# Decode attention, two blocks: all query weights first, output weights last, and a TensorE loop

## The chip, the cores and the metric

The kernel runs on one core of one Trainium2 chip. The metric is device time in microseconds, the median of several runs; lower is better.

## The reference, cut to what matters

Two blocks, A and B, of the same shape do the same work on their own inputs, and their results stand side by side in the output.

```python
B, Sq, D = 2, 1, 640
H, Sk, Dh = 32, 8192, 192          # bfloat16 everywhere
q = (x @ wq).reshape(B, Sq, H, Dh).transpose(0, 2, 1, 3)        # x: 2x1x640, wq: 640x6144
scores = einsum("bhqd,bhkd->bhqk", q, k_cache) * Dh ** -0.5      # k_cache: 2x32x8192x192
p = softmax(scores, axis=-1)
o = einsum("bhqk,bhkd->bhqd", p, v_cache)
block = o.transpose(0, 2, 1, 3).reshape(B, Sq, H * Dh) @ wo      # wo: 6144x640
out = concatenate([block_A, block_B], axis=-1)
```

Each K and each V cache has 201 MB; each wq and each wo has 7.86 MB. Every byte of them is read once, 836.77 MB in all, and there is one query per head.

## The kernel before

**Units.** Work goes by units. A unit is one batch element and two heads; block A has units 0 to 31 and block B units 32 to 63. Partitions 0 to 63 hold the first head, 64 to 127 the second, and each partition holds 128 positions of 192 values, so that one K (or V) load is 128 rows of 49,152 bytes, 6.29 MB. Two units, the two batch elements of a pair of heads, make a pair `hp`.

**Buffers and loads.** Three buffers `kv` take K and V in turn. SP issues all large loads from one queue in the order of the list `loads`: K of unit u+1 ahead of V of unit u, with the last two K ahead of the last three V. A load waits until the load three places before it has been used up: a K buffer is free after the fourth multiply of its unit (`("m", u, 3)`), a V buffer after its PV product (`("pv", u)`). One buffer `wbuf` holds the weights of eight heads at a time: wq of a window of eight heads (`sp_wq`, five rows of 3,072 bytes per partition) and wo of the window (`sp_wo`, four rows of 3,840 bytes per partition) alternate in it. They stand in SP's queue between the K loads, wq behind the sixth K of a window of eight units and wo behind the fourth of the next. The last window's wo comes as four loads after the last V.

**A unit's work.** TensorE makes the query of a unit, repeated over the partitions, with five matmuls (`pe_q`, L294), and ScalarE copies it to SBUF (`act_a0`, L277). VectorE multiplies K by the query in four chunks (`dve_mul`, L219). TensorE sums each product over 192 values as far as 16 with twelve matmuls against an identity (`pe_sum`, L302), VectorE does the rest (`dve_red`, L222) and takes the maximum (L228). GpSimd makes the maximum common to all partitions (L211). ScalarE takes the exponentials into `pb` (L252) with their sums in `rs`; GpSimd adds these over the partitions (L214) and VectorE inverts them (L236). TensorE multiplies by V with 64 matmuls, two positions at once (`pe_pv`, L312).

**Output.** For each pair, ScalarE copies the PV result out (`act_f1`, L261), TensorE turns it across partitions (`pe_f3`, L322), ScalarE scales it by the inverse sum (`act_f4`, L268), and for each window TensorE multiplies it by wo (`pe_f5`, L335), six matmuls a pair, each pair waiting for the one before it.

**Order.** The program is written out by hand: `put` places each operation in a slot and an order within it, and `_Stream.emit` writes each engine's list out in full, with the semaphore waits that remain. TensorE's slot u holds the sums of unit u and after them the PV product of unit u-1.

## Time and profile before

| what | value |
|---|---|
| time, median of 3 runs | 1975.02 us (1973.26 to 1975.65) |
| the profiled execution, first to last instruction (span) | 1972.4 us |
| moved by DMA | 837.99 MB, mean 425 GB/s |
| large loads, share of 16 DMA engines | 98.8% |
| program code, q8 | 66 packets, 1.08 MB |
| TensorE matmuls busy | 1576.7 us, 8448 of them |
| VectorE, ScalarE, GpSimd busy | 1067.3, 196.5 and 60.2 us |

The page comes from one execution, and its own time is the span; the 2.6 us between span and median lie outside the instructions. Times are from the span's start. GB/s and busy tenths are given for 40 equal slices of the span. In a group or timeline line the output stands left of the arrow and the inputs right of it, then the form and the count; a bracket gives the engine's idle time before it and who ended that. Beside the views, the trace holds a record of each DMA packet (start, length, bytes) and of each of the sixteen parts in which a load reports that it has landed.

### The profile page before, as it was taken

The page shows a single profiled execution, that of the slowest core. Times are in us where ns is not written, and L with a number is a line of the kernel's source. Part 1 is how long each engine was busy: PE and PEld are TensorE (multiplying, and loading weights), DVE is VectorE, ACT ScalarE, POOL GpSimd, SP SyncE. Part 2 cuts the span into 40 slices and gives each one's busy share as a digit, 9 for nine tenths or more (in the row PEclk, how much of TensorE's full clock was granted, in tenths as well). Part 3 has the DMA queues.
Part 4 walks back from the last instruction along what each step waited for, and adds up shares of the span by engine and source line. Part 5 has one row for each costly group of instructions (what it writes and reads, how often), then busy time and mean ns, then how long its engine had stood idle before and what let it go on. Part 6 is the DMA issues. An engine that isn't in the chain of part 4 may idle for free.

```text
span 1972.4 us, 18847 instructions
## 1 busy us (share of the span) xinstructions
PE 1576.7 (80%) x8448; PEld 773.3 (39%) x8448; DVE 1067.3 (54%) x772; ACT 196.5 (10%) x647; POOL 60.2 (3%) x145
## 2 busy tenths in 40 slices
PE   3887888878788788787887878878788777878769
PEld 1443434434344343343443434434344333443325
DVE  5664565545654555546556455464554655645570
ACT  0110110001000011000110101100011001110001
POOL 1000000000000000000000000000000000000000
PEclk9999998999999899998998989999999999999889
DMA  9999999999999999999999999999999999999996
GB/s 404 432 432 431 431 429 434 431 427 433 433 427 428 433 430 433 431 426 437 430 430 431 426 433 431 433 431 427 434 433 431 427 429 427 433 433 428 426 380 275
DMA packets 29345, 837.99 MB, mean 425 GB/s; under 512 B 3016, under 2 KB 3024, under 8 KB 12624
## 3 DMA queue, kind: packets, MB, share of 16 engines
q1 hardware_dynamic: 28676, 836.77, 98.8%
q8 instruction: 66, 1.08, 0.2%
q10 hardware_dynamic: 588, 0.01, 0.0%
q14 instruction: 15, 0.12, 0.0%
HBM read 836.77 MB, written 0.01 MB: 424 GB/s over the span
## 4 chain that ended last, share of the span: by engine, by line
DMA 50%; PE 28%; DVE 19%; issue 3%; ACT 0%; SPq 0%
DMA kv<-in_B_k_cache_dram 24%; DMA kv<-in_A_k_cache_dram 24%; PE ops L312 18%; DVE prod L219 17%; PE scps L302 9%; DVE sc L222 2%; DMA kv<-in_B_v_cache_dram 2%; PE outps L335 0%; PE qps L322 0%; PE qps L294 0%; DVE mp L228 0%; SPq L178 0%; ACT qbc L277 0%; DVE rcT L236 0%; ACT out_sb L282 0%
## 5 line engine op out<-in xcount | busy, mean ns | idle before, releaser
L219 DVE TENSOR_TENSOR prod<-kv,qbc 128x6144 bf16<-128x6144 bf16 x256 | 852.7, 3352 | 637.0 <-DMA kv<-in_B_k_cache_dram 320.3
L302 PE MATMUL scps<-prod,ident 128*128 128x512 bf16 x3072 | 775.2, 409 | 355.4 <-DVE prod L219 355.3
L312 PE MATMUL ops<-kv,pb 128*34 128x384 bf16 x4096 | 676.6, 326 | 2.2 <-DMA kv<-in_B_v_cache_dram 1.1
L302 PEld LDWEIGHTS scps<-prod,ident 128*128 128x128 bf16 x3072 | 301.3, 104 | 821.8 <-DVE prod L219 455.3
L312 PEld LDWEIGHTS ops<-kv,pb 128*34 128x34 bf16 x4096 | 395.6, 98 | 274.9 <-issue 15.5
L222 DVE TENSOR_REDUCE sc<-scps 128x32 f32<-128x512 f32 x256 | 175.8, 687 | 204.1 <-PE scps L302 204.1
L244 ACT ACTIVATE nb<-mg 64x1 f32<-64x1 f32 x128 | 25.7, 201 | 1314.3 <-POOL mg L211 1313.5
L294 PE MATMUL qps<-wbuf,xbc 128*128 128x384 bf16 x320 | 64.7, 334 | 34.4 <-ACT qbc L277 24.5
L252 ACT ACTIVATE pb<-sc,nb 64x128 bf16<-64x128 f32 x128 | 81.7, 638 | 31.9 <-PE ops L312 28.8
L211 POOL PARTITION_ALL_REDUCE mg<-mp x64 | 26.0, 406 | 1717.9 <-DVE mp L228 1717.9
L277 ACT ACTIVATE qbc<-qps 64x192 bf16<-64x192 f32 x128 | 41.6, 325 | 181.8 <-PE qps L294 180.6
L294 PEld LDWEIGHTS qps<-wbuf,xbc 128*128 128x128 bf16 x320 | 26.5, 99 | 69.8 <-ACT qbc L277 36.8
L261 ACT ACTIVATE o_sb<-ops 2x384 f32<-2x384 f32 (+1 forms) x66 | 31.1, 471 | 223.9 <-PE ops L312 223.5
L322 PEld LDWEIGHTS qps<-sel,o_sb 34*64 34x64 f32 x768 | 36.3, 171 | 13.6 <-issue 13.4
L322 PE MATMUL qps<-sel,o_sb 34*64 34x1 f32 x768 | 39.1, 225 | 0.0
L252 ACT ACTIVATION_READ_ACCUMULATOR pb<-sc,nb 64x1 f32 x128 | 38.6, 301 | 0.0
L228 DVE TENSOR_REDUCE mp<-sc 64x1 f32<-64x128 f32 x128 | 35.9, 280 | 3.1
L236 DVE RECIPROCAL rcT<-lall 64x1 f32<-64x1 f32 x128 | 20.1, 157 | 25.4 <-POOL lall L214 22.5
L214 POOL PARTITION_ALL_REDUCE lall<-rs x64 | 27.9, 436 | 157.6 <-ACT pb L252 157.6
L335 PE MATMUL outps<-wbuf,oTz 128*4 128x320 bf16 x192 | 31.3, 299 | 1.4
L335 PEld LDWEIGHTS outps<-wbuf,oTz 128*4 128x4 bf16 x192 | 13.7, 84 | 16.3 <-PE outps L335 8.9
L268 ACT ACTIVATE oTz<-qps,rcT 128x3 bf16<-128x3 f32 x64 | 13.7, 268 | 15.5 <-PE qps L322 14.7
(19 smaller groups left out, 15.8 us busy)
## 6 DMA issues: line engine op xcount, KB each, us to landing
kv<-in_A_k_cache_dram SPq DMA_DIRECT2D x32, 6144.0 KB, 30.3
kv<-in_A_v_cache_dram SPq DMA_DIRECT2D x32, 6144.0 KB, 30.1
kv<-in_B_k_cache_dram SPq DMA_DIRECT2D x32, 6144.0 KB, 30.5
kv<-in_B_v_cache_dram SPq DMA_DIRECT2D x30, 6144.0 KB, 30.4
kv<-in_B_v_cache_dram SPq DMA_DIRECT2D x3, 3072.0 KB, 13.0
wbuf<-in_A_wq_dram SPq DMA_DIRECT2D x4, 1920.0 KB, 33.3
wbuf<-in_A_wo_dram SPq DMA_DIRECT2D x4, 1920.0 KB, 33.1
wbuf<-in_B_wq_dram SPq DMA_DIRECT2D x4, 1920.0 KB, 32.9
```

Of the source, the lines that this page charges most:

```text
L214: return lambda eng: eng.partition_all_reduce(lall[u % 2][:], rs[u % 2][:], 128, bass.bass_isa.ReduceOp.add)
L219: return lambda eng: eng.tensor_tensor(prod[c % 2][:], t[:, c * TC:(c + 1) * TC, :], q, ALU.mult)
L222: return lambda eng: eng.tensor_reduce(sc[u % 2][:, c * TC:(c + 1) * TC], scps[c % 2][:], AXL.X, ALU.add)
L228: ins = eng.tensor_reduce(mp[u % 2][r, s:s + 1], sc[u % 2][r, :], AXL.X, ALU.max)
L252: ins = eng.activation(pb[u % 2][r, :, s::32], sc[u % 2][r, :].rearrange("p (j a) -> p j a", a=2), ACTF.Exp, bias=nb[u % 2][r, :], scale=s ...
L261: ins = eng.activation(o_sb[r, b0:b1, :], ops[hp % 2][r, b0:b1, a * Dh:(a + 1) * Dh], ACTF.Identity)
L277: ins = eng.activation(qbc[u % NQ][r, :], qps[r, s * Dh:(s + 1) * Dh], ACTF.Identity)
L294: ins = eng.matmul(qps[:, 0:QW], xbc[b][:, c, :], wq_t[:, c, off:off + QW], start=(c == 0), stop=(c == DC - 1))
L302: ins = eng.matmul(scps[c % 2][:], ident[:], prod[c % 2][:, :, j * DG:(j + 1) * DG], start=(j == 0), stop=(j == NJ - 1))
L312: ins = eng.matmul(ops[(u // B) % 2][0:MP, u % B, 0:QW], pb[u % 2][:, j, :], vv[:, j, :], start=(j == 0), stop=(j == TJ - 1))
L322: ins = eng.matmul(oTps[64 * s:64 * s + 64, 2 * i + b:2 * i + b + 1], o_sb[:, b, :].rearrange("p (r i) -> p i r", i=3)[:, i, :], sel[:, s: ...
L335: ins = eng.matmul(outps[0:4, 0:NH2], oTz[:, hp % NZ, i, 2 - 2 * half:6 - 2 * half], wo_t[:, hp % PW, i, half * NH2:(half + 1) * NH2], sta ...
```

## The change

- **wq first.** The whole wq of block A and that of block B are loaded at the start, each in one transfer, one row of 61,440 bytes per partition (`ld_wq`). They lie in one large tile `big`, in the place that the K/V buffers and the products take later. All 32 pairs' queries are made before the first unit: `pe_q` now makes both batch elements of a pair with five matmuls, VectorE (`dve_qx`) and ScalarE (`act_q`) copy them into `qall`. The first two K loads wait for block A's queries, the first V for all.
- **wo last.** wo comes in eight pieces (`pieces`, `ld_wo`) with rows of 30,720 bytes down to 2,560. The first, half of block A's, goes to the last K's buffer and stands in SP's queue ahead of the last V; the others follow the last V. K and V alternate to the end.
- **Outputs.** A unit's PV result is added up and scaled by VectorE and ScalarE and written over the unit's query in `qall`. The sums of the exponentials come from one small matmul (`pe_l`) in place of GpSimd's. At the end TensorE turns each block's outputs with 64 matmuls against `place` (`pe_turn`) and multiplies them by wo with 96 (`pe_out`).
- **Loop.** `_find` looks for the longest stretch of slots that repeats every six; TensorE's list has the slots 3 to 62 as a loop of ten turns, in which each wait is for a register times a step plus a constant. The slots before and after, and the other engines' lists, are written out.

The diff, cut to its core:

```diff
+    def emit(self, eng, period=None):
+        ops = self.resolve()
...
+        first, plen, reps, steps = self._find(ops, period)
+        self._emit(eng, ops[:first])
+        with eng.Fori(0, reps) as it:
+            self._emit(eng, ops[first:first + plen], it, steps)
+        self._emit(eng, ops[first + plen * reps:])
...
+    def _emit(self, eng, ops, it=None, steps=None):
+        for fn, need, has_sig, _ in ops:
+            for sid, (sem, val) in need.items():
+                eng.wait_ge(sem, val if it is None else it * steps[sid] + val)
...
-        wbuf = sb("wbuf", [128, DC * HW * Dh], BF16)
+        big = sb("big", [128, NBUF * BUFE + 2 * PRODE], BF16)
+        qall = sb("qall", [128, NU, Dh], BF16)
...
-        for u in (LASTU - 1, LASTU):
-            loads.remove(("k", u))
-            loads.insert(loads.index(("v", LASTU - 3)), ("k", u))
...
+        pieces = [
+            (0, 0, HWR, woA, [("m", LASTU, NCH - 1)]),
+            (0, HWR, WR, woA + HWR * D, [("s", LASTU, NCH - 1)]),
+            (1, 0, 16, b62 * BUFE, [("pv", LASTU - 1)]),
+            (1, 16, 32, b62 * BUFE + 16 * D, []),
+            (1, 32, 40, b63 * BUFE, [("pv", LASTU, 0)]),
+            (1, 40, 44, b63 * BUFE + 8 * D, []),
+            (1, 44, 46, b63 * BUFE + 12 * D, []),
+            (1, 46, 48, b63 * BUFE + 14 * D, []),
+        ]
...
+        def ld_wq(blk):
+            src = blocks[blk]["wq"].rearrange("(j c) n -> j (c n)", c=DC)
+            return dma(big[:, wq_off[blk]:wq_off[blk] + WQE], src, ("wq", blk))
+
+        def ld_wo(n):
+            blk, r0, r1, off, _ = pieces[n]
+            src = blocks[blk]["wo"].rearrange("(p i) n -> p (i n)", i=WR)
+            return dma(big[:, off:off + (r1 - r0) * D], src[:, r0 * D:r1 * D], ("wo", n))
...
+        def dve_qx(hp, s):
+            ri, ro = slice(64 * (1 - s), 64 * (1 - s) + 64), slice(64 * s, 64 * s + 64)
+            return lambda eng: eng.tensor_copy(qall[ro, B * hp + 1 - s, :], qps[hp % NCH][ri, s * Dh:(s + 1) * Dh])
...
+        def dve_rc(u):
+            return lambda eng: eng.reciprocal(rc[u % 2][:], ops[u % 2][0:2, QW:QW + 1])
+
+        def dve_ohi(u):
+            return lambda eng: eng.tensor_copy(o_hi[:], ops[u % 2][32:34, Dh:QW])
+
+        def dve_osum(u):
+            return lambda eng: eng.tensor_tensor(o_sum[:], ops[u % 2][0:2, 0:Dh], o_hi[:], ALU.add)
+
+        def act_of(u):
+            return lambda eng: eng.activation(qall[0:2, u, :], o_sum[:], ACTF.Identity, scale=rc[u % 2][:])
...
-                    ins = eng.matmul(qps[:, 0:QW], xbc[b][:, c, :], wq_t[:, c, off:off + QW],
+                    ins = eng.matmul(qps[hp % NCH][:, 0:QW], xbc[:, blk, c, :], wq_t[blk][:, c, off:off + QW],
...
+        def pe_l(u):
+            return lambda eng: eng.matmul(ops[u % 2][0:2, QW:QW + 1], rs[u % 2][:], ones[:], start=True, stop=True)
...
+        def pe_turn(hp):
+            def fn(eng):
+                for g in range(GP):
+                    s0 = 128 - 2 * GP * (hp % PPB) - g
+                    ins = eng.matmul(oTps[:, 0:B * WR], place[:, s0:s0 + 128],
+                                     qall[0:2, B * hp:B * hp + B, g * WR:(g + 1) * WR],
...
+                for i in range(r0, r1):
                     for half in range(2):
...
+                        ins = eng.matmul(outps[0:4, 0:NH2], oTz[blk][:, i, 2 - 2 * half:6 - 2 * half],
+                                         wo[:, i - r0, half * NH2:(half + 1) * NH2],
...
+            put("pe", u + 1, 2, pe_l(u), w0, ("l", u), ("l", u % 2))
...
+        for blk in range(NBLK):
+            S_sp.add(ld_wq(blk))
         for i, (kind, u) in enumerate(loads):
...
+            w = [done(i - NBUF)]
+            if i < 2:
+                w = [("pq", PPB - 1)]
+            elif i == 2:
+                w = [("pq", NP - 1)]
+            if (kind, u) == ("v", LASTU):
+                S_sp.add(ld_wo(0), waits=pieces[0][4])
+            for n, fn in enumerate(ld_kv(kind, u)):
+                S_sp.add(fn, waits=w if n == 0 else [])
+        for n in range(1, len(pieces)):
+            S_sp.add(ld_wo(n), waits=pieces[n][4])
...
-                S_pe.emit(eng)
+                S_pe.emit(eng, period=6)
```

TensorE's order after the loop is: the sums of unit 63, `pe_l` and PV of unit 62, block A's 64 turns, PV of unit 63, the first half of block A's products with wo, block B's first 60 turns, the second half of A's products, the last four turns, and block B's products as its pieces come.

## The prediction

> **What bounds the kernel now.** I read the page first, then the waits of the DMA queue, the chain in order of time, the landing and packet records of the transfers, and last the two ends in stages. The page says that the 16 DMA engines never rest:

> ```profile
> span 1972.4 us, 18847 instructions
> ...
> PE 1576.7 (80%) x8448; PEld 773.3 (39%) x8448; DVE 1067.3 (54%) x772; ACT 196.5 (10%) x647; POOL 60.2 (3%) x145
> ...
> GB/s 404 432 432 431 431 429 434 431 427 433 433 427 428 433 430 433 431 426 437 430 430 431 426 433 431 433 431 427 434 433 431 427 429 427 433 433 428 426 380 275
> ...
> q1 hardware_dynamic: 28676, 836.77, 98.8%
> q8 instruction: 66, 1.08, 0.2%
> ```

> The rate is flat at 426 to 437 GB/s and sags only in the last two slices. q8 is program code: 66 packets for 2 x 8448 TensorE records, so one packet per 256 instructions. No engine feeds a starving queue either; SP mostly waits for a buffer to come free:

> ```profile
> SPq L178 <- DVE prod L219: 1022.5, 64, 37.7
> SPq L178 <- PE ops L312: 855.3, 61, 18.1
> ```

> From issue to landing a K load takes 27.5 to 35 us in the chain, and a load alone would need 14.53 us of transfer and some 3 us around it, so about 10 us of queue are always ahead.

> ```profile
> 1.52 23.02 DMA kv<-in_A_k_cache_dram
> ...
> 1068.25 33.85 DMA kv<-in_B_k_cache_dram
> ...
> 1310.66 35.19 DMA kv<-in_B_k_cache_dram
> ```

> K loads land at 1102.1 and 1345.8: 243.7 us for eight units, that is 16 K/V loads, one wq and one wo load. In the trace's packet records a 49,152 B row takes 1.816 us on its engine; eight rows per engine give 14.53 us a load, and most landings are just that far apart. A load of wq (3,072 B rows) or wo (3,840 B) adds 4.82 us between landings. 16 x 14.53 + 2 x 4.82 = 242.1, so 1.6 us in every 243.7 is something else. It is the code: each q8 packet takes 1.06 us and stretches the row beside it from 1.82 to 2.3 us, about 1.55 us lost on one engine. The sixteen parts of one load land 1.5 us apart at load 1 and 11.7 us apart at load 121: about half of the engines take the code, and the slowest ones set when a buffer is full. 62 packets / 8 x 1.55 = 12.0 us. Check: the first K landed at 24.54; 24.54 + 121 x 14.53 + 14 x 4.82 = 1850.1, and load 121 landed at 1862.45, 12.3 later.

> The end is TensorE's. DMA has all but finished at 1956, and three PV products run in one row:

> ```profile
> 1921.83 31.38 PE L312 MATMUL ops<-kv,pb 128*34 128x384 bf16 x192
> ...
> 1970.17 0.43 ACT L282 ACTIVATE out_sb<-outps 4x320 bf16<-4x320 f32 x1 [2.74 <-PE outps L335]
> ```

> **The change, part by part.** I build the new span from its start.

> *Start, weights.* K's 24.54 is 14.53 for itself, 40 packets x 0.128 = 5.1 for wq, and 4.9 of start-up. A wq is now one transfer of 7.86 MB in 61,440 B rows. At the K rows' rate that is 8 x 2.27 = 18.16 us per engine: wq A lands at 4.9 + 18.16 = 23.1, wq B's data end at 40.8. The first K waits for `("pq", 15)`, the queries of block A. Their rows are:

> ```profile
> 9.90 1.78 PE L294 MATMUL qps<-wbuf,xbc 128*128 128x384 bf16 x5 [9.90 <-DMA wbuf<-in_A_wq_dram]
> ...
> 43.75 0.98 PE L294 MATMUL qps<-wbuf,xbc 128*128 128x384 bf16 x5
> ```

> Slow at first (0.32 us each), then 0.164 us from one to the next. 80 of them: 12 slow (3.9) + 68 x 0.164 (11.1) + waits 0.7 = 15.7, so pq 15 at 38.8; data follow an issue by 1.44 us (first issue 0.80, first packet 2.24), so at 40.3, before wq B is through. The two PSUM copies on DVE per pair are not in the trace: between L228's 0.28 and L222's 0.69 us; by size 0.35, so 0.7 a pair, under TensorE's 0.82. At 0.69 they would set the pace and K would start 5.7 us late. I take 0.5. First K: 40.8 + 14.53 + 0.45 (packet end to landing) + 0.5 = 56.3. Block B's queries end near 55.5, before the first multiply, with K of unit 1 still in flight, so the V load behind them loses nothing.

> *Middle.* Fourteen inserted loads (67.5 us) go; of those bytes, half are now at the start and half at the end. K of unit 63 is 125 loads later: 56.3 + 125 x 14.53 = 1872.6, plus code.

> *Code.* TensorE's slots 3 to 62 are one body run ten times: 6 x (48 + 64 + 1) matmuls, 1,356 records, 5.3 packets. Before it stand 439 matmuls, 3.4 packets. If the body stays in the engine, some 10 packets are read by then, at most two on one engine: 2.5 us. If it is read on every turn, 7 to 8 packets a turn with the cut blocks at both ends: 57 to 83 in all, 11 to 16 us; I take 13. The packets' durations repeat every eight (1.09, 1.09, 1.02, 1.03, 1.07, 1.07, 1.07, 1.10), which looks like eight places, and 8 x 256 = 2,048 holds 1,356. So I take "stays": **1875.1**. [...]

> *Hidden.* The branch and its register arithmetic lie in TensorE's idle time before a K (4.0 us in units near the end) and the 10 us of queue. Three small DVE operations a unit (at most 0.35 each) replace two reciprocals, inside 637 us of waiting for K; ACT (10%) and POOL (3%) lose evictions and 64 sums. [...] Each costs nothing while K loads set the pace, and its own length per unit otherwise.

> *End*, counted from K 63's landing. Its last multiply ends at +16.0 (14.3 to 16.6 in the chain's legs), and only then is wo's first half issued: SP stands there with V 63 queued behind it, while V 62 ends at +14.1. So DMA idles some 3.5 us. With 1.6 us to start, wo 0 runs to 26.7 (9.1), V 63's pieces land at 34.4, 38.1, 41.8, wo 1 at 50.9, the last piece at 70. TensorE: sums to 18.8, PV 62 to 29.3, 64 turning matmuls (new: L322 starts one each 0.049 us, L312 each 0.164; I take 0.07) to 33.8, PV 63 from 34.4 to 44.9. Then output products:

> ```profile
> 356.47 4.08 PE L335 MATMUL outps<-wbuf,oTz 128*4 128x320 bf16 x24
> ```

> Within a run of six they start 0.136 us apart, with a gap at each self-wait; the new ones have no such wait. 48 take 6.5 (51.4), 60 turns 4.2 (2.9 to 9.8), 48 more 6.5 (62.1), last turn and two evictions 1.3, 96 products 13.0 (76.4), eviction and store 2.3: **+78.7**. TensorE is last, not wo.

> Sum: 1872.6 + 2.5 + 78.7 = 1953.8 of span. The median is 2.6 above the span of the profiled execution (1975.02 against 1972.4), so **1957 us**, 0.9% less. Its own range is 1953 to 1963.

> **Rivals.** *Read on every turn*: the same sum with 13: 1964.3, so 1967. For it: no block was ever used twice in this trace, so nothing shows that one is kept. Against: the eights. *Each back branch refills all eight places*: 5.3 + 8 packets, ten turns, about 137: 26.5 us, span 1977.8, time 1980, slower. It passes the old span from 110 packets on. For it: reading ahead went on to the last 12 us of the kernel (a packet at 1960.8), where little code was left. Against: packets came one by one, 29 us apart, never in bursts. *The branch stalls TensorE past the queue's 10 us*, late PV, late K issue: at 15 us a turn 50 us, 2007. Against: a 16 KB packet takes 1.1 us, so even several in a row stay under it.

> **How the numbers follow.** Stays 0.54, read on every turn 0.33, refill 0.10, stall 0.03. About 0.2% (4 us) is what a measurement of this kernel can tell from no change; 1971 is that line. The first case is faster nearly whole (0.53). The second has 4 us of margin against unknowns of 6 at the start and 5 at the end: 0.21 faster, 0.09 no change, 0.03 slower. Refill: 0.02 no change, 0.08 slower. The stall is slower. Faster 0.74, same 0.12, slower 0.14. The range 1953 to 1973 takes in the second case and leaves out the last two.

> **What would show it.** Right: q8 well under 30 packets; K landings 14.5 us apart with hardly a wq or wo step; the first K landing near 56; GB/s of 434 in the middle slices; the last wo piece landing 6 us or more before TensorE's last product. Wrong: q8 at 60 packets or more (second case), above 110 (third), DVE waiting for one K much longer than the 15.1 us that is the longest now (fourth), or a gap of over 2 us between wq B and K.

## The result, and the profile after

The changed kernel took 1963.84 us (median of 4 runs, 1962.65 to 1964.02) against 1974.19 us (4 runs) for the kernel before: a ratio of 0.9946, 95% interval 0.9932 to 0.996. That is faster by 10.35 us. The forecast was 1957 in a range of 1953 to 1973; the sign and the range held, the middle was 6.8 us too low, and the gain was some 60% of the one forecast.

The page of the changed kernel, the same lines as before (q14 is code too, in packets of 8,192 bytes):

```profile
span 1962.0 us, 17861 instructions
...
PE 1527.6 (78%) x7781; PEld 744.5 (38%) x7781; DVE 1123.5 (57%) x901; ACT 160.3 (8%) x519; POOL 31.3 (2%) x80
...
GB/s 396 433 433 432 433 432 432 433 433 433 431 433 433 433 433 433 433 433 433 433 432 433 432 433 433 432 433 433 433 434 433 433 433 433 433 433 432 433 332 327
...
q1 hardware_dynamic: 20164, 836.77, 98.9%
q8 instruction: 13, 0.21, 0.0%
q14 instruction: 15, 0.12, 0.0%
```

Two things answer the forecast at once. q8 fell from 66 packets to 13, so the loop body is not read again on every turn. And the rate in the middle is an even 431 to 434 GB/s, where it was 426 to 437: no weights stand between K and V any more. The right edge has changed its form but not its sum: 332 and 327 in the last two slices, where before had 380 and 275. The queue is partly idle at the end as before, and now earlier.

SP's waits (total, times, longest) have kept their shape; each V load still waits for the multiplies of its unit, and each K load for a PV product:

```profile
SPq L235 <- DVE big L280: 997.9, 64, 29.6
SPq L235 <- PE ops L365: 812.2, 62, 13.1
```

In the chain of waits (start, length, what) the last K lands at 1852.76 + 28.05 = 1880.81. Of the pieces behind it the longest are one V load, one PV product and the output:

```profile
1852.76 28.05 DMA big<-in_B_k_cache_dram
1897.81 19.63 DMA big<-in_B_v_cache_dram
1917.49 12.21 PE ops L365 x64
```

TensorE's timeline shows the same place closer. The bracket is its idle time before the row:

```profile
1910.79 2.89 PE L374 MATMUL oTps<-qall,place 2*128 2x96 bf16 x64
...
1917.49 12.21 PE L365 MATMUL ops<-big,pb 128*34 128x384 bf16 x64 [3.69 <-DMA big<-in_B_v_cache_dram]
1929.63 6.68 PE L387 MATMUL outps<-big,oTz 128*4 128x320 bf16 x48
...
1946.59 13.20 PE L387 MATMUL outps<-big,oTz 128*4 128x320 bf16 x96 [0.74 <-ACT out_sb L327]
```

Short stretches of the end (behind the busy times of the five engines come the granted clock, the DMA share and GB/s) show why V 63 was late, and what TensorE met:

```profile
1884.00:1886.00 2.00, 1.75 (x5) 0.64 (x6) 2.00 (x2) 0.00 (x0) 0.00 (x0) 0.50 0.85 369
...
1888.00:1890.00 2.00, 2.00 (x6) 0.73 (x5) 0.41 (x1) 0.00 (x0) 0.00 (x0) 0.50 0.17 74
...
1896.00:1898.00 2.00, 0.90 (x5) 0.30 (x4) 2.00 (x2) 0.00 (x0) 0.00 (x0) 1.00 0.00 0
...
1915.00:1920.00 5.00, 2.51 (x8) 1.19 (x9) 0.00 (x0) 0.00 (x0) 0.00 (x0) 0.50 0.95 403
```

The rate falls from 369 to 74 GB/s and then to nothing until 1898. SP stands at the first half of wo, which waits for the last multiply of unit 63, and V 63 is queued behind it. That multiply is late itself, since unit 63's sums begin at a granted clock of 0.50 and VectorE waits for them. When V 63 does land, TensorE has been idle for 3.69 us, and the clock is at 0.50 again.

### The profile page after: what moved, and what is told of

It reads as the page before. It is cut to its first block, busy times and chain, and to the rows that moved or that the text cites. A ratio compares the mean times of both kernels' runs of the same rounds, so it can differ in the third digit from the quotient of the medians.

```text
span 1962.0 us, 17861 instructions
## 1 busy us (share of the span) xinstructions
PE 1527.6 (78%) x7781; PEld 744.5 (38%) x7781; DVE 1123.5 (57%) x901; ACT 160.3 (8%) x519; POOL 31.3 (2%) x80
## 3 DMA queue, kind: packets, MB, share of 16 engines
q1 hardware_dynamic: 20164, 836.77, 98.9%
HBM read 836.77 MB, written 0.01 MB: 426 GB/s over the span
## 4 chain that ended last, share of the span: by engine, by line
DMA 49%; PE 30%; DVE 20%; issue 0%; ACT 0%; SPq 0%
DMA big<-in_B_k_cache_dram 24%; DMA big<-in_A_k_cache_dram 22%; DVE big L280 17%; PE ops L365 17%; PE scps L352 11%; DVE sc L283 2%; DMA big<-in_B_wq_dram 2%; PE outps L387 1%; DMA big<-in_B_v_cache_dram 1%; PE scps L344 1%; PE ops L358 0%; PE oTps L374 0%; ACT out_sb L327 0%; SPq L235 0%; DVE mp L289 0%
## 5 line engine op out<-in xcount | busy, mean ns | idle before, releaser
L280 DVE TENSOR_TENSOR big<-big,qall 128x6144 bf16<-128x6144 bf16 x256 | 852.7, 3351 | 534.3 <-DMA big<-in_B_k_cache_dram 277.4
L352 PE MATMUL scps<-big,ident 128*128 128x512 bf16 x3072 | 782.2, 412 | 402.1 <-DVE big L280 402.1
L365 PE MATMUL ops<-big,pb 128*34 128x384 bf16 x4096 | 678.5, 327 | 3.7 <-DMA big<-in_B_v_cache_dram 3.7
L352 PEld LDWEIGHTS scps<-big,ident 128*128 128x128 bf16 x3072 | 304.0, 104 | 873.7 <-DVE big L280 497.8
L365 PEld LDWEIGHTS ops<-big,pb 128*34 128x34 bf16 x4096 | 396.0, 98 | 263.6 <-DMA big<-in_B_v_cache_dram 3.8
L344 PE MATMUL scps<-big 128*128 128x384 bf16 x160 | 31.1, 364 | 14.5 <-DMA big<-in_A_wq_dram 11.0
L270 DVE CAST qall<-scps 64x192 bf16<-64x192 f32 x64 | 22.7, 355 | 19.5 <-PE scps L344 16.8
L303 ACT ACTIVATE qall<-o_sum,rc 2x192 bf16<-2x192 f32 x64 | 29.0, 454 | 18.1 <-DVE o_sum L300 16.4
L344 PEld LDWEIGHTS scps<-big 128*128 128x128 bf16 x160 | 17.1, 108 | 28.2 <-DMA big<-in_A_wq_dram 11.1
L387 PE MATMUL outps<-big,oTz 128*4 128x320 bf16 x192 | 26.6, 299 | 0.7 <-ACT out_sb L327 0.7
L294 DVE RECIPROCAL rc<-ops 2x1 f32<-2x1 f32 x64 | 10.0, 156 | 28.3 <-PE ops L365 26.3
L274 ACT ACTIVATE qall<-scps 64x192 bf16<-64x192 f32 x64 | 20.8, 325 | 34.4 <-DVE qall L270 32.2
L297 DVE COPY o_hi<-ops 2x192 f32<-2x192 f32 x64 | 22.3, 349 | 2.0
L387 PEld LDWEIGHTS outps<-big,oTz 128*4 128x4 bf16 x192 | 16.1, 85 | 10.7 <-issue 1.2
L358 PEld LDWEIGHTS ops<-ones,rs 128*2 128x2 f32 x128 | 5.5, 82 | 26.8 <-issue 26.7
## 6 DMA issues: line engine op xcount, KB each, us to landing
big<-in_A_k_cache_dram SPq DMA_DIRECT2D x32, 6144.0 KB, 29.2
```

The lines of the kernel that those rows point to most:

```text
L270: return lambda eng: eng.tensor_copy(qall[ro, B * hp + 1 - s, :], qps[hp % NCH][ri, s * Dh:(s + 1) * Dh])
L280: return lambda eng: eng.tensor_tensor(prod[c % 2], t[:, c * TC:(c + 1) * TC, :], q, ALU.mult)
L303: return lambda eng: eng.activation(qall[0:2, u, :], o_sum[:], ACTF.Identity, scale=rc[u % 2][:])
L344: ins = eng.matmul(qps[hp % NCH][:, 0:QW], xbc[:, blk, c, :], wq_t[blk][:, c, off:off + QW], start=(c == 0), stop=(c == DC - 1))
L352: ins = eng.matmul(scps[c][:], ident[:], prod[c % 2][:, :, j * DG:(j + 1) * DG], start=(j == 0), stop=(j == NJ - 1))
L365: ins = eng.matmul(ops[u % 2][0:MP, 0:QW], pb[u % 2][:, j, :], vv[:, j, :], start=(j == 0), stop=(j == TJ - 1))
```

## The experiments

All are edits of the changed kernel; "over" means the time from the first K's landing (the last of its sixteen parts) to the last K's beyond 125 x 14.53 = 1816.25 us. The experiments ran on three chips. The kernel before ran beside them and took 1974.4 to 1974.9 us (medians), and each ratio is to it. Differences between two experiments are a few us, about as much as the runs scatter, so their medians carry a verdict only where the landings and rows of the two traces say the same.

### The loop undone

```diff
-                S_pe.emit(eng, period=6)
+                S_pe.emit(eng)
```

> The changed kernel with TensorE's list written out in full, nothing else. Theory (code): the loop saves the reading of program code, because its body stays in the engine. Then about 60 packets on q8 in place of 13; each costs one of about eight DMA engines 1.55 us, so by unit 63's K some 48 / 8 x 1.55 = 9 us more on the slowest engine, less where VectorE's own code (7 x 0.97 us, on one engine) sat on another one: that K lands 5 to 9 us later than 1880.8, span 1967 to 1971, time 1969 to 1973. Rival (weights): the gain of the change is from long rows and from wq and wo taken out of the middle, and the loop is only neutral: K of unit 63 within 1 us of 1880.8, time within 1 us of 1963.8.

Measured: 1969.39 us (8 runs), ratio 0.9972 [0.9962, 0.9983]. The page:

```profile
span 1967.3 us, 17500 instructions
...
q8 instruction: 61, 1.00, 0.2%
```

61 packets are 2 x 7781 records at 256 a packet. The last K landed 10.96 us over, against 6.82 in the changed kernel, and the first K 1.1 us later. So the loop is worth 4.1 us by the landings and 5.5 by the medians, of 10.35, and TensorE's code stretches the stream as read from the trace of before.

### A body too long to stay

```diff
-                S_pe.emit(eng, period=6)
+                S_pe.emit(eng, period=12)
```

> The changed kernel with TensorE's loop over twelve units, five turns. The body has 2,712 matmul and weight-load records, 10.6 code packets. Theory (eight places): TensorE keeps eight packets of code, so this body cannot stay and is read again on every turn: 5 x 11 or 12 + 7, some 62 to 67 packets on q8, and K of unit 63 lands as late as in the kernel written out, time 1969 to 1973. Rival (any body stays): about 18 packets on q8, time within 1 us of 1963.8.

Measured: 1970.66 us (10 runs), ratio 0.998 [0.997, 0.9989]; over 12.5 us. The page:

```profile
span 1970.0 us, 17851 instructions
...
q8 instruction: 70, 1.15, 0.2%
```

The body of twelve units has 12 x (48 + 64 + 2) x 2 = 2,736 records, 10.7 packets, and was read on every turn; the one of six, 1,368 records and 5.3 packets, was read once (13 packets). Expected were 2,712 and 1,356, which take each `pe_l` as one matmul; in the traces it stands as two. The forecast's second case thus exists, from somewhere between 5.3 and 10.7 packets on. The eight places that it read from the packets' durations lie between; where exactly the line is was not tried.

### More code on VectorE

Ten memsets of one column per unit, of a tile that nothing reads, on VectorE.

```diff
+            for e in range(10):
+                i = 10 * u + e
+                put("dve", u, 23, (lambda i: lambda eng: eng.memset(pad[:, i:i + 1], 0.0))(i), [], None)
```

> The changed kernel with ten small memsets a unit more on VectorE (640 in all, into a spare tile, off every path). Theory (code): VectorE's own code is read in 8,192-byte packets of 128 instructions, always through the same DMA engine, and each read sets that engine back 0.97 us (0.32 of its own and 0.65 on the K/V row beside it); seven of them stand as steps of 15.5 us between landings in place of 14.53. 640 instructions are five packets more: K of unit 63 lands 4.9 us later, span about 1967, time about 1968.7. VectorE's own time for them, some 0.1 us each or 1 us a unit, lies in its wait for K (534 us in all) and costs nothing. Rival: the steps have nothing to do with VectorE's code, and the time stays within 1 us of 1963.8.

Measured: 1968.52 us (5 runs), ratio 0.9969 [0.9955, 0.9983]. The page:

```profile
span 1967.9 us, 18501 instructions
...
q8 instruction: 13, 0.21, 0.0%
q14 instruction: 20, 0.16, 0.0%
```

640 instructions are five packets of 128: 15 became 20. Over: 11.9 us, 5.0 more than without them. Twelve landing steps of some 15.5 us stand here, one behind each of VectorE's packets within the K and V stream. The changed kernel has seven such packets. Five of them show as steps of 15.5; the first two lie behind TensorE's code, which had already delayed another DMA engine (steps of 15.01 and 15.46 that end at 160 and 190 us). VectorE has 534 us of waiting for K in the changed kernel, so the memsets' own time can't do this. It is their code: a packet of 0.32 us stretches the row beside it from 1.82 to 2.48 us, 0.97 in all. That the losses add up in the landings (12 x 0.97 = 11.6 of the 11.9) says that they fall on the same DMA engine.

### wo's first half behind the last V

```diff
-            if (kind, u) == ("v", LASTU):
-                S_sp.add(ld_wo(0), waits=pieces[0][4])
...
-        for n in range(1, len(pieces)):
+        for n in range(len(pieces)):
```

> The changed kernel with the first half of block A's wo issued behind the last V instead of ahead of it. Theory (the queue's head): SP's 29.6 us wait for the last multiply holds the last V back; without it V 63's pieces land at about L+22, +25.5 and +29.2 (L = landing of unit 63's K) in place of +36.6, +40.3, +43.9; TensorE then runs from PV 62 to the end with hardly a pause: PV 63 ends near L+43.5 (now +48.9), the end at L+76 (now +81.2): 5 us less, time about 1959. Rival: TensorE's products with wo, which now find their first half landed, wait for it instead, and the time stays within 1.5 us of 1963.8.

Measured: 1958.81 us (4 runs), ratio 0.9924 [0.9907, 0.994], span 1957.2. TensorE's timeline:

```profile
1912.60 0.19 PE L358 MATMUL ops<-ones,rs 128*2 128x1 f32 x2
1912.72 10.57 PE L365 MATMUL ops<-big,pb 128*34 128x384 bf16 x64
1923.22 6.68 PE L387 MATMUL outps<-big,oTz 128*4 128x320 bf16 x48
```

PV 63 starts without a wait and takes 10.57. The end from the last K's landing is 76.6 us (1957.2 - 1880.65) instead of 81.2. Of these 4.6 us, 0.8 lies ahead of the place of the edit: the last multiply ended 15.8 us behind its K instead of 16.6. "Half of block A's ahead of the last V" costs some 4 us; the transfer that was to fill the queue stopped it.

### The first products ahead of PV 63

```diff
-        where = {0: (E1, 4), 1: (E2, 4)}
+        where = {0: (E1, 2.9), 1: (E2, 4)}
```

> The changed kernel with the first half of block A's output products (turns and 48 products) put ahead of the last PV pass in TensorE's order instead of behind it. Theory: TensorE is the last engine of the end (its last product ended 7 us behind the last weight's landing) and has 3.7 us of idle time just before the last V lands, so moving 2.7 us of turns and 6.6 us of products into and before this stretch ends the span 4 to 6 us earlier: span 1956 to 1958, time about 1959; the granted clock of the last PV pass, which started from idle, should then be up and the pass take 10.5 us instead of 12.2. Rival: the first half of the weights lands too late for that (1910.2 against the last V at 1917.5 to 1924.8), so that the PV pass is only pushed back and the output weights that wait for it come later: no gain, 1962 to 1966.

Measured: 1958.57 us (4 runs), ratio 0.9915 [0.9898, 0.9931], span 1957.7. TensorE's timeline:

```profile
1911.44 8.36 PE L387 MATMUL outps<-big,oTz 128*4 128x320 bf16 x48 [0.32 <-ACT oTz L324]
1919.72 10.57 PE L365 MATMUL ops<-big,pb 128*34 128x384 bf16 x64
```

The wait for V 63 is now full of products, and the end is 77.3 us, 3.9 less. Not all of this is the edit's: in this profile the granted clock stayed at 1.00 under unit 63's sums (it was 0.50 in the changed kernel), and unit 63's last multiply ended 14.4 us behind its K instead of 16.6. That is 2.2 of the 3.9, ahead of the place of the edit. The time agrees with the theory, the split does not prove it.

### wq in short rows

```diff
-            return dma(big[:, wq_off[blk]:wq_off[blk] + WQE], src, ("wq", blk))
+                for w in range(4):
+                    ins = eng.dma_start(dst[:, w], src[:, w]).then_inc(s, 16)
```

> The changed kernel with each block's query weights again brought in four transfers of 3,072-byte rows instead of one of 61,440-byte rows; all else as in the changed kernel. Theory: the start is a chain of transfers, so the longer loading lies on the path whole. By the rows of the kernel before, a 3,072-byte row takes 0.125 to 0.128 us against 2.27 for 61,440 bytes, which is 20 rows at 2.5 to 2.56; 16 partitions' rows on each of 16 engines, 8 a block, are 2 blocks x 8 x 0.23 to 0.29 = 3.7 to 4.7 us more. The first whole K lands 62 us into the span instead of 57.7, the span is 1966 to 1967, the time about 1968. Rival: the queries hide it (TensorE is the last before the first K is issued), and the time stays at 1964.

Measured: 1964.87 us (4 runs), ratio 0.9951 [0.9934, 0.9967], span 1963.0: 1 us over the changed kernel. The theory's 4 us failed; the time is the rival's. In the packet records the short rows held each DMA engine 40.9 us instead of 37.4, 3.5 more. But K's first rows, right behind, took at most 2.48 us each, where 23 of the changed kernel's first 128 took 2.0 to 4.1; with the long rows an engine loses 1.15 us there, with the short ones 0.13. The first K landed at 58.58 against 57.74. Over all eleven profiles of the changed kernel and its edits it landed between 56.5 and 58.8, so the long rows' part is no more than that scatter. The rival's reason did not hold either: the first K was issued at 38.52, and wq's last row ended at 42.56, so the queries were not the last. Why K's first rows are slow behind long rows is open.

### The last K one place ahead

As in the kernel with all wo behind the last V, and:

```diff
+        loads.remove(("k", LASTU))
+        loads.insert(loads.index(("v", LASTU - 2)), ("k", LASTU))
...
-                put("pe", u, 0, pe_sum(c),
+                put("pe", u if u < LASTU else u - 1, 0 if u < LASTU else 1, pe_sum(c),
```

> The changed kernel with the last K loaded one place earlier (ahead of the last but two V instead of behind it), the sums of the last unit ahead of the PV pass before, and all output weights behind the last V, block A's first half in the place of the last but two V. Theory: what is left at the end after the last transfer of V is only the PV pass and the output, and the DMA gap of 9 to 10 us before the first half of wo goes; the last V lands 1902.6 / 1906.3 / 1909.9 us into the span, the last output weight near 1947, the last product near 1950: span about 1952, time about 1954, 10 below the changed kernel and 5 below the kernel that only moved the first half of wo behind the last V (1958.8). Rival: what is bounded there is the transfers that wait for the PV passes, not the K; then it is no better than that kernel, 1957 to 1960.

Measured: 1960.58 us (4 runs, 1958.40 to 1963.34), ratio 0.9929 [0.9912, 0.9945], span 1957.7. The theory's 1954 failed, and the time is near the rival's 1957 to 1960, but not for its reason. The transfers came as expected (V 63's pieces at 1902.0, 1905.6 and 1909.3, the last wo at 1945.9), and from unit 63's sums on TensorE waited for none. TensorE's timeline:

```profile
1875.14 7.43 PE L355 MATMUL scps<-big,ident 128*128 128x512 bf16 x24 [5.61 <-DVE big L283]
1884.03 2.76 PE L355 MATMUL scps<-big,ident 128*128 128x512 bf16 x12 [1.46 <-DVE big L283]
1887.90 2.76 PE L355 MATMUL scps<-big,ident 128*128 128x512 bf16 x12 [1.10 <-DVE big L283]
1890.59 0.19 PE L361 MATMUL ops<-ones,rs 128*2 128x1 f32 x2
1890.72 10.57 PE L368 MATMUL ops<-big,pb 128*34 128x384 bf16 x64
```

VectorE needs 20.7 us a unit with its waits for TensorE's sums (first multiplies at 1851.08 and 1871.75), more than the 14.5 us between the two K. PV 61 stands behind unit 63's sums until 1890.7, and from there to the last product TensorE is never idle but for 0.74 us. The end is TensorE's work, not the transfers.

### VectorE in a loop

The same kernel, with ScalarE's copy of each unit's query in one of two places, so that VectorE's addresses repeat:

```diff
-            q = qall[:, u, :].unsqueeze(1).broadcast_to([128, TC, Dh])
+            q = qcur[u % 2][:].unsqueeze(1).broadcast_to([128, TC, Dh])
...
+        def act_qc(u):
+            return lambda eng: eng.activation(qcur[u % 2][:], qall[:, u, :], ACTF.Identity)
...
-                S_dve.emit(eng)
+                S_dve.emit(eng, period=6)
```

> The kernel with the last K ahead, and VectorE's instructions as a loop over six units too: ScalarE copies each unit's query to one of two fixed places, so that every VectorE address repeats after six units. Theory: what still delays the K and V stream in the changed kernel is VectorE reading its own instructions (seven times, 0.97 us each, on the one DMA engine that all landings wait for); in a loop of some 100 instructions they are read about once, so the last K lands 6 to 7 us earlier, the 2.48 us rows beside 8,192-byte packets are gone, span 1945 to 1946, time about 1948. ScalarE's 64 more small copies add at most one code packet of its own. Rival: the waits on a register's value and the branch back delay VectorE's multiplies, or the loop is read again on every turn: as with the last K ahead alone (1954) or slower.

Measured: 1956.39 us (4 runs), ratio 0.9902 [0.9886, 0.9919], span 1956.0. The page:

```profile
q8 instruction: 18, 0.29, 0.1%
q14 instruction: 9, 0.07, 0.0%
```

The code half of the theory held: six of VectorE's seven packets in the stream and the steps of 15.5 us are gone, and to V 62's landing the stream is 1.9 us over instead of 7.2. Of these 5.3 us, 1.6 went into a later first K (58.22 against 56.63), and V 62 landed 3.7 us earlier. The end gave 2.0 of that back: unit 63's first multiply waited 2.1 us for the copy of its query, which stood behind unit 62's exponentials on ScalarE. So the time expected, 1948, did not come. VectorE's timeline:

```profile
1870.08 6.63 DVE L284 TENSOR_TENSOR big<-big,qcur 128x6144 bf16<-128x6144 bf16 x2 [2.10 <-ACT qcur L310]
```

### The same loop, the last K in its old place

All wo behind the last V, VectorE in its loop, and the copy ahead of the exponentials on ScalarE:

```diff
-            put("act", u - 1, 100 if u == 0 else -1 if u == 1 else 5, act_qc(u), ...
+            put("act", u - 1, 100 if u == 0 else -1, act_qc(u), ...
```

> The kernel that moved only the first half of block A's output weights behind the last V (1958.8 us), with VectorE's instructions as a loop over six units and ScalarE's copy of each unit's query; the last K in its old place. Theory: the seven delays of 0.97 us of VectorE's own code go, the last K lands 6 to 7 us earlier behind the same first K (in the last kernel with this loop the 125 steps took 1.6 us over 125 x 14.53 instead of 6.9), and the end, which TensorE carries from the last K on, follows whole: 125 steps in 1817 to 1818.5, span 1951 to 1953, time 1953 to 1955. Rival: what VectorE's loop saves is lost again at the end, as it seemed with the last K ahead (1956.4): 1956 to 1959.

Measured: 1954.56 us (4 runs, 1952.37 to 1957.92), ratio 0.9896 [0.9879, 0.9912]; 4.25 less than without VectorE's loop. The profiled run is the slowest of the four, span 1956.2. The last K was 1.86 us over instead of 7.15, as expected; the first K landed 0.95 later, within the scatter. The end was 79.9 us, not 76.6: PV 63 took 13.38. TensorE's timeline, then the stretch in which it began:

```profile
1905.44 3.32 PE L378 MATMUL oTps<-qall,place 2*128 2x96 bf16 x64
1908.69 0.19 PE L362 MATMUL ops<-ones,rs 128*2 128x1 f32 x2
1908.81 13.38 PE L369 MATMUL ops<-big,pb 128*34 128x384 bf16 x64
```

```profile
1908.00:1913.00 5.00, 5.00 (x26) 2.62 (x24) 0.00 (x0) 0.58 (x2) 0.00 (x0) 0.50 1.00 430
```

The granted clock is 0.50 here too, though TensorE had not been idle. By the trace's clock records it fell at 1907.7, while the 64 turns ran.

### The turns ahead

The same, with the turns of all pairs but the last two at the ends of units 61 and 62 in TensorE's order:

```diff
-                put("pe", slot if not lastp else E2, order if not lastp else 5, pe_turn(hp),
+                early = hp < NP - 2
+                put("pe", LASTU - 2 + blk if early else E2, 9 if early else 0 if not lastp else 5, pe_turn(hp),
...
-        put("act", E1, 2, act_ot(0), ...
+        put("act", LASTU - 2, 9, act_ot(0), ...
```

> The same, and the turns of the outputs, all but those of the last four units, moved in TensorE's order from behind the last PV passes to the ends of units 61 and 62, where TensorE waits for VectorE. Theory: from the last K on TensorE is the bound (it stands idle some 5 us in the last 70), so the 2.89 + 2.6 us of turns that lie there come off whole: span about 1947, time about 1949. Rival: then the output weights' transfers become the last (the last of them landed 9 us before TensorE's last product): gain of 2 us or less.

Measured: 1949.65 us (4 runs, 1948.58 to 1950.39), ratio 0.9876 [0.9859, 0.9892], span 1946.8; the fastest of all, 24.7 us below the kernel before. TensorE's timeline:

```profile
1876.86 2.55 PE L378 MATMUL oTps<-qall,place 2*128 2x96 bf16 x56
1879.51 6.91 PE L356 MATMUL scps<-big,ident 128*128 128x512 bf16 x24
...
1905.18 10.57 PE L369 MATMUL ops<-big,pb 128*34 128x384 bf16 x64
1915.69 6.68 PE L391 MATMUL outps<-big,oTz 128*4 128x320 bf16 x48
...
1923.55 6.68 PE L391 MATMUL outps<-big,oTz 128*4 128x320 bf16 x48 [0.91 <-DMA big<-in_A_wo_dram]
```

The 56 turns fill the time in which TensorE waited for VectorE, and the end from the last K is 70.8 us (1946.84 - 1876.07). Against the 76.6 with wo behind the last V that is 5.8 less, where 5.5 of turns were moved; by the medians of this kernel and the one above it is 4.9. Part of that can be the clock: it stayed at 1.00 under PV 63 here (1905 to 1916), and PV 63 took 10.57 instead of 13.38. No run parts the two. A transfer is waited for again, wo's second half for 0.91 us: the two limits of the end now nearly meet.

## Why the prediction was right, and where its sizes were off

The sum was 56.3 + 1816.3 + 2.5 + 78.7 = 1953.8; the profiled execution had 57.7 + 1816.3 + 6.8 + 81.2 = 1962.0. The time alone does not show that the right case was picked: 1963.84 lies just above the 1953 to 1963 of "stays", and nearer to the 1967 of "read on every turn". The 13 packets decide, and the wide range took in terms that were too small.

- **Start: right but for 1.4 us.** wq A landed at 22.5 (forecast 23.1), the first K was issued at 37.65 (38.8, with data at 40.3), wq B landed at 41.02. VectorE's copies took 355 ns (0.35 by size) and stayed under TensorE's pace. "K 14.53 + 0.45" failed: its first rows took up to 4.1 us. The 1.4 us lie inside the scatter of this landing (56.5 to 58.8).
- **Code, TensorE's part: right.** "Stays" was the case; nine packets by unit 63's K for the "some 10" forecast, 13 in all, none between 301 and 1908 us. Where VectorE's code is in a loop too, the last K is still 1.9 us over, against the 2.5 forecast. The body of 10.7 packets was read again, as in the forecast's second case (70 packets); the one of 5.3 took turn after turn without a packet. So 1,368 records stayed, 2,736 did not.
- **Code, the term that was mis-sized.** "At most two on one engine: 2.5 us" counted TensorE's code alone. The page of before has a second queue of code, and it was passed over at 0.12 MB:

```profile
q14 instruction: 15, 0.12, 0.0%
```

The changed kernel has 15 there too. Seven of them are VectorE's, within the stream, and delay their DMA engine by 0.97 us each, 6.8 of the 6.82. More VectorE code brought 5.0 us more, VectorE's loop took 5.3 away: this cause is shown from both sides. The two do not add up: with TensorE's 61 packets (61 / 8 x 1.55 = 11.8 by the forecast's rule) the loss is 10.96, not 11.8 + 6.8. By these numbers the slowest DMA engine counts, and it covered VectorE's share while TensorE's code was read; so the loop took away 4.1 us where the forecast had 12.0 - 2.5 = 9.5.
- **Middle: right.** Steps of 14.53 wherever there is no code; no inserted load. The branch, `pe_l` (0.19 us a unit) and the small VectorE operations cost nothing that can be seen: the longest wait of VectorE for K was 10.1 us, 15.1 before.
- **End: mechanism right, 2.5 us too short.** The order was as worked out: SP stands at wo, the gap in DMA, TensorE last and 7 us behind the last weight (1959.8 against 1952.6; "6 us or more"). Turns 0.045 us each (0.07), 48 products 6.7 (6.5). The steps that failed lie before V 63. The last multiply ended at +16.6 (+16.0) behind sums at half clock. wo 0 landed 12.8 us after its issue at 1897.44, where 1.6 + 9.1 = 10.7 was forecast: its first row on each engine took 1.6 to 2.2 us instead of 1.14. V 63 so landed at +36.6, +40.3 and +44.0 (+34.4, +38.1, +41.8), and PV 63 took 12.2 (10.5) at a clock that the forecast had left at full. PV 63 so ended at +48.9 instead of +44.9, and the shorter turns gave 1.5 us of these 4 back. "DMA idles some 3.5 us" held for the DMA engine that was last (3.1); V 62's first part landed 9.2 us before its last, so others stood idle for up to 12 us.
- **From span to median** 3.2 us were added with rounding; it was 1.8. The 2.6 compared the span of one execution with the median of others; in every run on record with both, the time is 1.7 to 1.9 above its own span.

The rivals: *read on every turn* and *refill* did not come (13 packets), and no turn stalled TensorE. Of the 10.35 us gained, the loop has 4 to 5.5; the other 5 to 6 are the weights' and outputs' new places together, after the 4 us that wo's first half costs where it stands. No run took these places apart further. The packet records hold a candidate: wq's and wo's rows held a DMA engine 80.2 us before (41.0 and 39.2) and 75.0 after (37.4 and 37.6), 5.2 less, by longer rows. But where wq came in short rows again, 1 us of its 3.5 was lost, no more than the scatter, and wo's rows were not tried; so how much of the 5.2 reaches the end stays open.

## What to carry to other kernels

Where one stream of transfers is the bound, count every engine's code in the trace, not the largest: each of VectorE's seven packets here delayed the landings behind it by 0.97 us, and TensorE's loop paid because its body was not read again (13 packets on q8 in place of 61). A transfer put into a waiting queue "to fill it" has to be free to start at that point; here what stood behind it paid, some 4 us. And at the end of a kernel look for work that is ready long before, such as the turns here: putting it into earlier idle time was worth some 5 us here, as much as the loop.
